# Retention attention with a PReLU feed-forward on one core: opening and block 1's units in another order

## The chip, the cores and the metric

The kernel runs on one core of a Trainium2 chip. Its engines are TensorE (PE, with weight loads shown apart as PEld), VectorE (DVE), ScalarE (ACT), GpSimd (POOL) and SyncE (SP); each works through its own instructions in order and waits on semaphores for the others. The metric is the device time of one execution in microseconds (us).

## The reference

Attention without softmax, with a decaying state, for 4 batches, 8 heads, 768 positions and 64 elements per head; its output, 3072 tokens by 512, goes through a feed-forward of width 2048 with a PReLU between.

```python
for t in range(S):                      # q, k, v: (4, 8, 768, 64), fp32
    state = gamma * state + outer(k[:, :, t], v[:, :, t])
    y[:, :, t] = (1 / sqrt(64)) * (q[:, :, t] @ state)
x = y.transpose(0, 2, 1, 3).reshape(3072, 512)
h = x @ w_in                            # (512, 2048)
g = maximum(h, 0) + alpha * minimum(h, 0)
out = g @ w_out                         # (2048, 512)
```

## The kernel before

The sequence is cut into chunks of 128 positions. A **unit** w is two chunks (256 positions) of four heads of one batch; `g = w % 2` is the half of the heads. There are 24 units in six **blocks** of four; the four units of a block give 512 tokens of x, which are the input of one feed-forward.

For a unit: `load` issues three transfers of 256 KB on SP's queue (k, q, v). `prep` multiplies k and q with decay factors into kdq (in the first two blocks k on DVE, q on POOL; unit 3's k on POOL too). `turn` transposes kdq in eight PE instructions into a PSUM tile (trb), and ACT copies it to kq; `cast_v` lets ACT convert v to vx. `scores` multiplies keys with queries into the PSUM tile sc (16 small PE instructions), `masked` lets DVE apply the causal mask (m). `state_sums` forms the chunk's sum of k times v (st), `state` adds the decayed state (ss, tg on DVE). `within` multiplies m with v into the PSUM tile y, followed by the products with the carried state that lie in the same row half; it ends with a tiny DVE memset that only tells that they are through. `finish` adds the carried products of the other half, which wait for that memset, and ACT copies y into xT. A `visit(old, new)` is within(old), scores and state_sums(new), finish(old), masked and state(new). From block 2 on, DMA transposes give kq instead of `turn`.

The feed-forward of a block is `ffn1`, 64 dense PE instructions of 128x512: 16 tiles (hps) of four steps hp, steps 0 and 1 reading the heads of g = 0 and steps 2 and 3 those of g = 1; each finished tile goes through ACT (hm) and DVE (gt). Then `ffn2`, again 64 dense instructions (ops): four tiles of 16 steps, each copied by ACT and stored. `tick(gen, m)` issues m of them, so that visits of the next block stand between them.

The order is written by hand (`manual_schedule`): every engine takes its instructions as the program's text issues them. PSUM tiles come from four tags: f and p with two buffers each, s (scores) and y with one of two banks each; a new tile waits until the old one's readers are done. `busy(m)` issues m products of ones (idle on PE) that nobody reads.

The opening is the work on block 0's four units, ahead of any dense work: loads, prep, turn and so on, with `get_wi` and `get_wo` on POOL's queue fetching the weights in four pieces each (win, wout). The loads of blocks 1 and 2 are issued after that; the first of them waits until the third piece of w_out has landed (`held`). In the opening, the loop for w = 1, 2, 3 runs busy(8), scores(w), state_sums(w), turn(w+1), finish(w-1), masked(w), state(w), within(w). Then come ffn1(0), the state sums of the later chunks of units 2 and 3, and ffn2(0) with block 1's turns and visits between its ticks.

Of the kernel before, what the change touches and what calls it, by code (L numbers as in the profile page):

```python
# [9 lines left out]
FP = mybir.dt.float32  # L10
# [8 lines left out]
def kernel(  # L19
# [15 lines left out]
    nc = tc.nc  # L35
    B, H, S, D = q.shape
    d_model, d_ff = moe_w_in.shape
    NFT = d_ff // 128
# [47 lines left out]
    alpha_sb = sbp.tile([NFT, 128], FP, tag="alpha", name="alpha")  # L86
    warm = sbp.tile([128, 128], FP, tag="warm", name="warm")[:, 0:1]
    ones = sbp.tile([128, 256], F16, tag="ones", name="ones")[:, 0:128]
    oma_sb = sbp.tile([128, 128], FP, tag="oma", name="oma")[:, 0:NFT]
    w_in_all = sbp.tile([128, NP, d_ff], F16, tag="win", name="win")  # L90
    w_out_all = sbp.tile([128, NFT, d_model], F16, tag="wout", name="wout")
# [43 lines left out]
    def load(w, which="kqv"):  # L135
        u, g, b, c3 = place(w)
        t = staged.setdefault(w, {})
        for nm in which:
            src = {"k": k, "q": q, "v": v}[nm]
            t[nm] = sbp.tile([128, 4, 2 * D], FP, tag=f"{nm}s", bufs=8, name=f"{nm}s{w}")  # L140
            ins = nc.sync.dma_start(
                out=t[nm],
                in_=src[b, 4 * g : 4 * g + 4, TU * c3 : TU * c3 + TU, :].rearrange(
                    "h (p a) d -> p h (a d)", a=2
                ),
            )
            if held:
                behind(ins, held.pop(), "loads of the second block after the weights")
# [34 lines left out]
    def busy(m):  # L183

        ips = ps("idle", "f")
        for _ in range(m):
            nc.tensor.matmul(  # L187
                out=ips[:, 0:128], lhsT=ones, rhs=ones, start=True, stop=True
            )

    def cast_v(w):
        nc.scalar.activation(  # L192
            out=prepped[w][2], in_=v_ins.pop(w), func=COPY, bias=0.0, scale=1.0
        )

    def turn(w, tag, fill=0, v_first=False):
        kdq, kq, vx = prepped[w]
        flat = kdq.rearrange("p k z r d -> p (k z r d)")
        trb = ps("trb", tag, 1024, F16)
        for i in range(8):  # L200
            if i == 4 and fill:
                busy(fill)
            nc.tensor.transpose(  # L203
                out=trb[:, 128 * i : 128 * i + 128],
                in_=flat[:, 128 * i : 128 * i + 128],
                identity=ident,
            )
        if v_first:
            cast_v(w)
        nc.scalar.activation(  # L210
            out=kq.rearrange("p b i -> p (b i)"),
            in_=trb[:, 0:1024],
            func=COPY,
            bias=0.0,
            scale=1.0,
        )
        if not v_first:
            cast_v(w)

    DIAG = [(0, 0), (1, 1), (0, 1), (1, 0)]  # L220

# [67 lines left out]
    def carried(w, y, started, same, after=None):  # L289
        u, g, b, c3 = place(w)  # L290
        kq = live[w][1]
        for x in range(2):
            for r in range(2):
                c = r if same else 1 - r
                if c3 + c == 0:
                    continue
                ins = nc.tensor.matmul(  # L297
                    out=y[half(x), 256 + 256 * c + 128 * r : 384 + 256 * c + 128 * r],
                    lhsT=tgs[2 * u + c, g][half(r), x, :],
                    rhs=kq[half(r), 4 + 2 * x : 6 + 2 * x, half(c)],  # L300
                    start=(c, x) not in started,
                    stop=(same == (c == r)),
                    skip_group_check=True,
                )
                started.add((c, x))
                if after is not None:
                    behind(ins, after, "the other row half wrote this bank")
                    after = None
        return ins

    def within(w):
        u, g, b, c3 = place(w)
        vx, m2 = live[w][2:4]
        y = ps("y", "y", 1024, FP, 1)
        started = set()
        for r in range(2):
            for a in range(2):
                for c, x in DIAG:
                    nc.tensor.matmul(  # L319
                        out=y[half(x), 256 + 256 * c + 128 * r : 384 + 256 * c + 128 * r],  # L320
                        lhsT=vx[half(c), 2 * r + x, a, :],
                        rhs=m2[half(c), 2 * r + x, a, :],
                        start=(c, x) not in started,
                        stop=(a == 1 and c3 + c == 0),
                        skip_group_check=True,
                    )
                    started.add((c, x))
        last = carried(w, y, started, True)
        done = nc.vector.memset(warm[0:1], 0.0)  # L329
        behind(done, last, "tells that the products within the chunks are through")  # L330
        live[w].append((y, started, done))

    def finish(w):
        u, g, b, c3 = place(w)
        y, started, done = live[w].pop()
        carried(w, y, started, False, done)
        live.pop(w)
        n, i = divmod(u, 2)
        if w % WB == 0:
            xT[n] = sbp.tile([128, 2, 4, 2, 128], F16, tag="xT", bufs=2, name=f"xT{n}")  # L340
        nc.scalar.activation(  # L341
            out=xT[n][:, g, 2 * i : 2 * i + 2].rearrange("p c r (i a) -> p (c r) i a", a=2),
            in_=y[:, 256:768].rearrange("p (s a i) -> p s i a", a=2, i=64),
            func=COPY,
            bias=0.0,
            scale=1.0,
        )
# [15 lines left out]
    def prelu(gt, ft, hps, lo, hi, hm):  # L363
        nc.vector.scalar_tensor_tensor(  # L364
            out=gt[:, ft, lo:hi],
            in0=hm,
            scalar=oma_sb[:, ft : ft + 1],
            in1=hps,
            op0=MULT,
            op1=ADD,  # L370
        )

    def minus(hps):
        hm = sbp.tile([128, TB], FP, tag="hm", bufs=3, name="hm")
        nc.scalar.activation(out=hm, in_=hps, func=RELU, bias=0.0, scale=-1.0)  # L375
        return hm

    def ffn1(n, order="spyfSpYf"):
        gt = sbp.tile([128, NFT, TB], F16, tag="gt", bufs=2, name=f"gt{n}")
        gts[n] = gt  # L380
        banks = Banks(order)
        for ft in range(NFT):
            hps = banks.next("hps")
            for hp in range(NP):
                nc.tensor.matmul(  # L385
                    out=hps,
                    lhsT=w_in_all[:, hp, 128 * ft : 128 * ft + 128],
                    rhs=xT[n][:, hp // 2, :, hp % 2, :],
                    start=(hp == 0),
                    stop=(hp == NP - 1),  # L390
                )
                if hp == NP - 1:
                    prelu(gt, ft, hps, 0, TB, minus(hps))
                yield

    def ffn2(n, parts=1, order="f"):
        gt = gts.pop(n)
# [30 lines left out]
    nc.scalar.dma_start(out=tab, in_=tab_h.ap())  # L428
    nc.scalar.dma_start(out=mi, in_=mi_h.ap())
    nc.scalar.dma_start(out=alpha_sb, in_=moe_alpha.rearrange("(ft p) -> ft p", p=128))  # L430
    for w, which in ((0, "kqv"), (1, "kq"), (2, "kq"), (1, "v"), (3, "kq"), (2, "v"), (3, "v")):
        load(w, which)
    nc.vector.memset(warm, 0.0)  # L433
    nc.scalar.activation(out=warm, in_=warm, func=RELU, bias=0.0, scale=-1.0)

    wi = moe_w_in.rearrange("(hp p) d -> p hp d", p=128)
# [9 lines left out]

    busy(34)
    prep(0, opening=True)
    turn(0, "f", 12)
    prep(1, opening=True)  # L450
    busy(16)
    scores(0)
    state_sums(0)
    masked(0)
    aps = ps("aps", "f")
    nc.tensor.transpose(out=aps[:, 0:NFT], in_=alpha_sb, identity=tab[0:NFT, ALT : ALT + NFT])
    prep(2, opening=True)
# [121 lines left out]
```

## Time and profile before

| | us |
|---|---|
| median of 3 runs | 225.86 (224.89 to 225.87) |
| the profiled execution | 225.53 |
| its span in the trace | 223.8 |
| mean granted PE clock | 0.969 of full |
| PE busy | 210.0 (94%) |
| DVE busy | 128.7 (58%) |
| ACT busy | 99.0 (44%) |
| POOL busy | 58.2 (26%) |

The profile is that of one execution. Times in it count from the span's start. In a timeline row stand the start, the length, the engine, the line, the operation, what is written and read, and in brackets how long the engine had been idle and what ended that. An engine name with a q (SPq, POOLq) is the engine's queue issuing a transfer. In the rows of the DMA view the last number is the time from issue to landing. The busy time of PE includes the drain of each instruction, so that 64 dense instructions show 380 ns each while they follow each other 216 ns apart.

### The profile page before, as it was taken

The numbers are of one execution on the slowest core, as the hardware profiler recorded it, in microseconds if no ns is written. First come the engines' busy times: TensorE is split into PE (matmuls) and PEld (weight loads), VectorE is DVE, ScalarE is ACT, GpSimd is POOL, SyncE is SP. The second block draws the span as 40 slices with busy tenths as digits, with TensorE's granted clock in tenths as the row PEclk, the third lists the DMA queues.
The fourth block names the chain that finished last, engine by engine and source line by source line (L and its number), as shares of the span: only waits on it lengthen the run. The fifth ranks groups of instructions, "written<-read, shape, count | busy, mean of one in ns | idle before, by whom it ended". The sixth has DMA issues, their size and how long they took to land.

```text
span 223.8 us, 5215 instructions
## 1 busy us (share of the span) xinstructions
PE 210.0 (94%) x2183; PEld 107.1 (48%) x2183; DVE 128.7 (58%) x226; ACT 99.0 (44%) x162; POOL 58.2 (26%) x69
## 2 busy tenths in 40 slices
PE   8666899999789999999999999999999999999993
PEld 8555544446434454444455444455444555444441
DVE  1653268955558896338874468936188773388000
ACT  2533256435656722266621376423376332576121
POOL 1593000369604580434502244400000000000000
PEclk9995589999999999999999999999999999999999
DMA  6959999999549969399427599031450012100112
GB/s 200 347 109 206 205 194 231 314 321 316 185 107 248 274 178 210 130 242 238 124 70 214 100 219 317 26 94 51 115 124 0 0 50 96 48 0 0 50 61 79
DMA packets 62935, 34.08 MB, mean 152 GB/s; under 512 B 18736, under 2 KB 59840, under 8 KB 62912
## 3 DMA queue, kind: packets, MB, share of 16 engines
q1 hardware_dynamic: 58368, 29.37, 48.3%
q0 software_dynamic: 4224, 4.19, 11.5%
q8 instruction: 17, 0.28, 0.5%
q10 hardware_dynamic: 320, 0.19, 0.3%
q14 instruction: 6, 0.05, 0.1%
HBM read 27.45 MB, written 6.29 MB: 151 GB/s over the span
## 4 chain that ended last, share of the span: by engine, by line
PE 89%; DVE 5%; ACT 3%; issue 0%; DVEq 0%
PE hps L385 38%; PE ops L406 36%; PE idle L187 4%; PE y L319 4%; PE sc L233 3%; DVE m L268 3%; PE trb L203 2%; PE y L297 2%; ACT kq L210 1%; PE st L257 1%; DVE tg L286 1%; ACT xT L341 1%; DVE kdq L158 1%; ACT vx L192 0%; DVE ss L283 0%
## 5 line engine op out<-in xcount | busy, mean ns | idle before, releaser
L364 DVE SCALAR_TENSOR_TENSOR gt<-hm,oma,hps 128x512 f16<-128x512 f32 x96 | 71.7, 747 | 32.1 <-ACT hm L375 21.7
L406 PE MATMUL ops<-wout,gt 128*128 128x512 f16 x384 | 89.2, 380 | 0.0
L385 PE MATMUL hps<-xT,win 128*128 128x512 f16 x384 | 85.8, 385 | 0.2 <-ACT xT L341 0.2
L375 ACT ACTIVATE hm<-hps 128x512 f32<-128x512 f32 x96 | 57.3, 597 | 28.6 <-PE hps L385 28.6
L385 PEld LDWEIGHTS <-win 128*128 128x128 f16 x384 | 37.9, 99 | 46.6 <-issue 2.6
L406 PEld LDWEIGHTS <-gt 128*128 128x128 f16 x384 | 35.2, 98 | 39.7
L268 DVE TENSOR_TENSOR m<-sc,mi 128x1024 f16<-128x1024 f32 x24 | 29.3, 1223 | 8.6 <-PE sc L233 6.7
L158 POOL TENSOR_TENSOR kdq<-qs,tab 128x512 f16<-128x512 f32 x24 | 25.8, 1075 | 31.5 <-DMA qs<-in_q_dram 30.3
L341 ACT ACTIVATE xT<-y 128x512 f16<-128x512 f32 x24 | 14.3, 597 | 43.4 <-PE y L297 40.7
L158 POOL TENSOR_TENSOR kdq<-ks,tab 128x512 f16<-128x512 f32 x17 | 17.9, 1054 | 52.1 <-DMA ks<-in_k_dram 43.0
L415 ACT ACTIVATE os<-ops 128x512 f32<-128x512 f32 x24 | 14.3, 597 | 33.4 <-PE ops L406 33.4
L329 DVE MEMSET warm<- 1x1 f32 x24 | 1.4, 59 | 29.6 <-PE y L297 29.6
L319 PE MATMUL y<-m,vx 64*64 64x128 f16 x384 | 10.5, 229 | 5.2 <-ACT xT L341 3.8
L210 ACT ACTIVATE kq<-trb 128x1024 f16<-128x1024 f16 x8 | 8.2, 1023 | 13.8 <-PE trb L203 13.8
L297 PE MATMUL y<-kq,tg 64*64 64x128 f16 x160 | 12.0, 237 | 1.8 <-DVE tg L286 1.2
L319 PEld LDWEIGHTS <-vx 64*64 64x64 f16 x384 | 6.8, 110 | 14.1 <-issue 11.0
L286 DVE TENSOR_TENSOR tg<-ss,tab 128x128 f16<-128x128 f32 x32 | 11.4, 355 | 1.1
L187 PE MATMUL idle<-ones 128*128 128x128 f16 x102 | 10.4, 278 | 1.1 <-DVE warm L433 1.1
L233 PE MATMUL sc<-kq 64*64 64x128 f16 x384 | 10.3, 224 | 0.3 <-ACT kq L210 0.2
L178 POOL CAST vx<-vs 128x512 f16<-128x512 f32 x16 | 9.8, 615 | 0.3 <-DMA vs<-in_v_dram 0.3
L283 DVE TENSOR_TENSOR ss<-tg,st 128x128 f32<-128x128 f16 x32 | 9.0, 282 | 1.5
L187 PEld LDWEIGHTS <-ones 128*128 128x128 f16 x102 | 8.8, 129 | 1.6 <-DVE warm L433 1.1
(22 smaller groups left out, 59.8 us busy)
## 6 DMA issues: line engine op xcount, KB each, us to landing
ks<-in_k_dram SPq DMA_DIRECT2D x24, 256.0 KB, 4.3
qs<-in_q_dram SPq DMA_DIRECT2D x24, 256.0 KB, 4.2
vs<-in_v_dram SPq DMA_DIRECT2D x24, 256.0 KB, 4.4
out_dram<-os SPq DMA_DIRECT2D x24, 256.0 KB, 2.3
win<-in_moe_w_in_dram POOLq DMA_DIRECT2D x4, 512.0 KB, 9.0
wout<-in_moe_w_out_dram POOLq DMA_DIRECT2D x4, 512.0 KB, 16.7
kq<-kdq SPq DMA_TRANSPOSE x16, 3.6
mi<-mi_const ACTq DMA_DIRECT2D x1, 128.0 KB, 2.9
```

The source lines that it names most:

```text
L158: eng.tensor_tensor(out=kdq[:, kind].rearrange("p z r d -> p r z d"), in0=src.rearrange("p (r x) (a d) -> p r (x a) d", a=2, x=2), in1=tab ...
L187: nc.tensor.matmul(out=ips[:, 0:128], lhsT=ones, rhs=ones, start=True, stop=True)
L233: nc.tensor.matmul(out=sc[half(c), at : at + 128], lhsT=kq[half(r), 2 * x + a, half(c)], rhs=kq[half(r), 4 + 2 * x : 6 + 2 * x, half(c)], ...
L268: nc.vector.tensor_tensor(out=m2.rearrange("p s a i -> p s (a i)"), in0=sc.rearrange("p (s n) -> p s n", n=256), in1=mask.unsqueeze(1).to_ ...
L297: ins = nc.tensor.matmul(out=y[half(x), 256 + 256 * c + 128 * r : 384 + 256 * c + 128 * r], lhsT=tgs[2 * u + c, g][half(r), x, :], rhs=kq[ ...
L319: nc.tensor.matmul(out=y[half(x), 256 + 256 * c + 128 * r : 384 + 256 * c + 128 * r], lhsT=vx[half(c), 2 * r + x, a, :], rhs=m2[half(c), 2 ...
L341: nc.scalar.activation(out=xT[n][:, g, 2 * i : 2 * i + 2].rearrange("p c r (i a) -> p (c r) i a", a=2), in_=y[:, 256:768].rearrange("p (s ...
L364: nc.vector.scalar_tensor_tensor(out=gt[:, ft, lo:hi], in0=hm, scalar=oma_sb[:, ft : ft + 1], in1=hps, op0=MULT, op1=ADD,)
L375: nc.scalar.activation(out=hm, in_=hps, func=RELU, bias=0.0, scale=-1.0)
L385: nc.tensor.matmul(out=hps, lhsT=w_in_all[:, hp, 128 * ft : 128 * ft + 128], rhs=xT[n][:, hp // 2, :, hp % 2, :], start=(hp == 0), stop=(h ...
L406: nc.tensor.matmul(out=opss[tq], lhsT=gt[:, ft, 128 * tq : 128 * tq + 128], rhs=w_out_all[:, ft, :], start=(ft == 0), stop=(ft == NFT - 1),)
L415: nc.scalar.activation(out=os_sb, in_=opss[tq], func=COPY, bias=0.0, scale=1.0)
```

## The change

The order in which instructions are issued changes, and with it the waits; the result is formed from the same products. In the opening the loads go unit by unit; scores(w) are issued ahead of within(w - 1) (unit 1's scores follow within(0) directly); the first piece of w_in is fetched ahead of unit 3's prep; cast_v is called apart from turn, mostly after finish; unit 2's `within` tells ACT instead of DVE that it is through (`teller`, a copy of one element). The fillers number 78 instead of 102. ffn1(0) begins with the steps of g = 0 of its first four tiles (`lead=4`): two of these inside within(3) (`mid`), two before finish(3), four after it; its tiles take their banks in another order. Block 1 gets other tick counts: units 6 and 7 are prepared later, turn(7) stands ahead of visit(5, 6), and unit 7 is finished with three dense instructions left. The code of blocks 2 to 5 is as before.

```diff
@@ load order @@
-    for w, which in ((0, "kqv"), (1, "kq"), (2, "kq"), (1, "v"), (3, "kq"), (2, "v"), (3, "v")):
-        load(w, which)
+    for w in range(WB):
+        load(w)
@@ turn no longer calls cast_v @@
-    def turn(w, tag, fill=0, v_first=False):
+    def turn(w, tag, fill=0):
...
-        if v_first:
-            cast_v(w)
...
-        if not v_first:
-            cast_v(w)
@@ within @@
-    def within(w):
+    def within(w, mid=None, teller=None):
...
+        if mid:
+            mid()
         last = carried(w, y, started, True)
-        done = nc.vector.memset(warm[0:1], 0.0)
+        if teller is None:
+            done = nc.vector.memset(warm[0:1], 0.0)
+        else:
+            done = teller.activation(
+                out=word[0:1], in_=word[0:1], func=COPY, bias=0.0, scale=1.0
+            )
@@ ffn1 @@
-    def ffn1(n, order="spyfSpYf"):
+    def ffn1(n, order="spyfSpYf", lead=0):
...
-        for ft in range(NFT):
-            hps = banks.next("hps")
-            for hp in range(NP):
...
+        hpss = {}
+        steps = [(ft, hp) for ft in range(lead) for hp in range(2)]
+        steps += [(ft, hp) for ft in range(lead) for hp in range(2, NP)]
+        steps += [(ft, hp) for ft in range(lead, NFT) for hp in range(NP)]
+        for ft, hp in steps:
+            if hp == 0:
+                hpss[ft] = banks.next("hps")
...
@@ opening @@
-    turn(0, "f", 12)
+    turn(0, "f", 8)
+    cast_v(0)
     prep(1, opening=True)
-    busy(16)
+    busy(12)
...
     prep(2, opening=True)
+    get_wi(0)
...
     turn(1, "f")
+    cast_v(1)
     within(0)
     prep(3, opening=True, k_on=nc.gpsimd)
-    for i in range(4):
+    for i in range(1, 4):
         get_wi(i)
...
-    for w in range(1, WB):
-        busy(8)
-        scores(w)
-        state_sums(w, (0,) if w > 1 else None)
-        if w + 1 < WB:
-            turn(w + 1, "f")
-        finish(w - 1)
-        masked(w)
-        state(w, (0,) if w > 1 else None)
-        within(w)
+    scores(1)
+    turn(2, "f")
+    finish(0)
+    cast_v(2)
+    state_sums(1)
+    masked(1)
+    state(1)
     busy(8)
+    scores(2)
+    within(1)
+    masked(2)
+    turn(3, "f")
+    finish(1)
+    cast_v(3)
+    state_sums(2, (0,))
+    state(2, (0,))
+    busy(8)
+    scores(3)
+    within(2, teller=nc.scalar)
+    masked(3)
+    state_sums(3, (0,))
+    finish(2)
+    state(3, (0,))
+    busy(8)
+    gen = ffn1(0, "ffspypSY", 4)
+    within(3, mid=lambda: tick(gen, 2))
+    tick(gen, 2)
     finish(3)
-    busy(8)
...
-    for _ in ffn1(0):
+    for _ in gen:
         pass
@@ block 1 @@
-    for w in range(WB, 2 * WB):
-        prep(w, opening=True)
-    tick(gen, 30)
-    turn(4, "p", v_first=True)
+    prep(4, opening=True)
+    prep(5, opening=True)
+    tick(gen, 21)
+    cast_v(4)
+    turn(4, "p")
+    tick(gen, 6)
+    visit(None, 4)
+    prep(6, opening=True)
+    tick(gen, 3)
+    cast_v(5)
+    turn(5, "p")
     tick(gen, 5)
-    visit(None, 4)
+    visit(4, 5)
+    prep(7, opening=True)
+    tick(gen, 3)
+    cast_v(6)
+    turn(6, "p")
+    tick(gen, 5)
+    cast_v(7)
+    turn(7, "p")
+    visit(5, 6)
     tick(gen, 8)
-    turn(5, "p", v_first=True)
-    tick(gen, 6)
-    visit(4, 5)
-    tick(gen, 1)
-    turn(6, "p", v_first=True)
-    tick(gen, 5)
-    visit(5, 6)
-    turn(7, "p", v_first=True)
-    tick(gen, 5)
     visit(6, 7)
+    tick(gen, 8)
+    within(7)
+    tick(gen, 2)
+    finish(7)
     for _ in gen:
         pass
-    visit(7, None)
```

More of the change, by code (lines that the diff above doesn't have):

```diff
@@ L88 @@
     ones = sbp.tile([128, 256], F16, tag="ones", name="ones")[:, 0:128]
+    word = sbp.tile([128, 128], FP, tag="word", name="word")[:, 0:1]
     oma_sb = sbp.tile([128, 128], FP, tag="oma", name="oma")[:, 0:NFT]
@@ L381, in ffn1 @@
         banks = Banks(order)
-        for ft in range(NFT):
-            hps = banks.next("hps")
-            for hp in range(NP):
[L385 to L394, printed above, removed]
+        hpss = {}
[5 more added lines that the diff above has]
+                hpss[ft] = banks.next("hps")
+            nc.tensor.matmul(
+                out=hpss[ft],
+                lhsT=w_in_all[:, hp, 128 * ft : 128 * ft + 128],
+                rhs=xT[n][:, hp // 2, :, hp % 2, :],
+                start=(hp == 0),
+                stop=(hp == NP - 1),
+            )
+            if hp == NP - 1:
+                prelu(gt, ft, hpss[ft], 0, TB, minus(hpss.pop(ft)))
+            yield
     def ffn2(n, parts=1, order="f"):
@@ L430 @@
     nc.scalar.dma_start(out=alpha_sb, in_=moe_alpha.rearrange("(ft p) -> ft p", p=128))
-    for w, which in ((0, "kqv"), (1, "kq"), (2, "kq"), (1, "v"), (3, "kq"), (2, "v"), (3, "v")):
-        load(w, which)
+    for w in range(WB):
+        load(w)
     nc.vector.memset(warm, 0.0)
+    nc.vector.memset(word, 0.0)
     nc.scalar.activation(out=warm, in_=warm, func=RELU, bias=0.0, scale=-1.0)
```

## The prediction, made before the changed kernel had run

> **What bounds the kernel now.** I read the engine shares first, then the chain of waits, then the waits of the tensor engine, and last the timeline of the first 65 us.
>
> ```profile
> span 223.8 us, 5215 instructions
> PE 210.0 (94%) x2183; PEld 107.1 (48%) x2183; DVE 128.7 (58%) x226; ACT 99.0 (44%) x162; POOL 58.2 (26%) x69
> 26.36 15.53 PE hps L385 x64
> 42.26 6.58 PE ops L406 x30
> 48.84 0.45 PE trb L203 x8
> 64.95 13.56 PE hps L385 x62
> 110.62 0.43 PE ops L406 x2
> 128.62 13.81 PE hps L385 x64
> 206.09 13.83 PE ops L406 x64
> ```
>
> The columns of the chain are start, length, what. From 64.95 us to the end the chain is the tensor engine (PE) back to back: 64 dense products take 13.81 us, 0.216 us each, whether of the first (hps) or second (ops) product. Nothing there is touched, so the change is worth what it does before 64.95. Two products of block 1's first tile had already run when the 62 began, so dense work of block 1 starts, in effect, at 64.95 - 2 x 0.216 = 64.5. I call that the mark. Behind it lie 223.8 - 64.5 = 159.3 us.
>
> Ahead of the mark two things cost time. A later block needs 128.62 - 110.62 = 18.0 us from its first ops to the next hps; block 0's ffn2 needs 64.5 - 42.26 = 22.2. Four transposition groups (0.45 each, block 1 only) explain 1.8, so about 2.4 us are waits. And the dense work does not start before 26 us.
>
> ```profile
> PE y L319 <- ACT xT L341: 3.8, 2, 1.9
> PE y L319 <- DVE m L268: 1.4, 3, 1.0
> PE trb L203 <- DVE tg L286: 1.3, 1, 1.3
> 9.20:12.60 3.40, 2.02 (x67) 1.68 (x66) 3.03 (x8) 1.54 (x2) 2.91 (x3) 1.00 0.97 286
> 12.60:16.00 3.40, 1.46 (x40) 1.12 (x41) 1.65 (x5) 2.03 (x3) 3.40 (x6) 1.00 0.37 53
> 22.90:26.30 3.40, 2.96 (x41) 2.51 (x42) 0.93 (x4) 0.68 (x2) 0.00 (x0) 0.50 1.24 206
> 26.30:29.70 3.40, 3.40 (x10) 1.20 (x9) 0.75 (x1) 0.60 (x1) 0.00 (x0) 0.50 1.22 195
> 29.70:33.10 3.40, 3.40 (x18) 1.50 (x17) 2.28 (x4) 2.39 (x4) 0.00 (x0) 1.00 1.22 198
> ```
>
> First the waits (total, times, longest), then the windows: after the window's length come the busy times of PE, PEld, DVE, ACT and POOL, then the granted PE clock, the DMA share and GB/s. The longest waits are `within` (y L319) for xT on ScalarE (ACT). After the thin window 12.6 to 16.0 (PE busy 1.46 us) the clock is granted at 0.50, and it comes back only after a window that is all dense work: 10 dense matmuls started from 26.3 to 29.7, against 18 in the next window. That is (18 - 10) x 0.216 = 1.7 us lost.
>
> **The opening, step by step.** These rows of the timeline (start, length, engine, line, what) carry it:
>
> ```profile
> 6.84 0.69 DVE L158 TENSOR_TENSOR kdq<-ks,tab 128x512 f16<-128x512 f32 x1 [2.28 <-DMA ks<-in_k_dram]
> 7.71 1.43 SPq L141 DMA_DIRECT2D vs<-in_v_dram  x2
> 9.15 1.04 POOL L158 TENSOR_TENSOR kdq<-qs,tab 128x512 f16<-128x512 f32 x1 [0.46 <-DMA qs<-in_q_dram]
> 9.27 1.47 DVE L158 TENSOR_TENSOR kdq<-ks,tab 128x512 f16<-128x512 f32 x1
> 10.66 0.28 DVE L286 TENSOR_TENSOR tg<-st,tab 128x128 f16<-128x128 f32 x1
> 10.68 1.04 POOL L158 TENSOR_TENSOR kdq<-ks,tab 128x512 f16<-128x512 f32 x1 [0.49 <-DMA ks<-in_k_dram]
> 11.17 0.62 PE L187 MATMUL idle<-ones 128*128 128x128 f16 x8
> 11.72 0.42 PE L233 MATMUL sc<-kq 64*64 64x128 f16 x16
> 12.85 1.02 ACT L210 ACTIVATE kq<-trb 128x1024 f16<-128x1024 f16 x1 [2.07 <-PE trb L203]
> 13.78 0.62 ACT L192 ACTIVATE vx<-vs 128x512 f16<-128x512 f32 x1
> 14.29 0.59 ACT L341 ACTIVATE xT<-y 128x512 f16<-128x512 f32 x1
> 14.93 0.42 PE L319 MATMUL y<-m,vx 64*64 64x128 f16 x16 [1.94 <-ACT xT L341]
> 15.89 0.54 PE L233 MATMUL sc<-kq 64*64 64x128 f16 x16
> 21.36 0.64 PE L233 MATMUL sc<-kq 64*64 64x128 f16 x16
> vs<-in_v_dram SPq DMA_DIRECT2D x1, 256.0 KB, 5.3
> L268 DVE TENSOR_TENSOR m<-sc,mi 128x1024 f16<-128x1024 f32 x24 | 29.3, 1223 | 8.6 <-PE sc L233 6.7
> L364 DVE SCALAR_TENSOR_TENSOR gt<-hm,oma,hps 128x512 f16<-128x512 f32 x96 | 71.7, 747 | 32.1 <-ACT hm L375 21.7
> ```
>
> Before, each unit is a closed loop: scores, transposes of the next, kq, vx, xT, and only then `within`, behind which the next scores stand. sc of unit 2 starts at 15.89, of unit 3 at 21.36.
>
> 1. Load order. k and q of units 2 and 3 move one slot back on SyncE's queue. Slots are 0.76 apart: POOL's q2 is released by its load at 9.15 and k3, two slots on, at 10.68. q2 now arrives near 9.9. DVE's k2 multiply took 1.47 beside POOL's q2 and 0.69 alone (6.84); now it runs 9.35 to 10.05, ahead of POOL. Bounds: nothing to -0.78 on the first tg; I take -0.6. So `within(0)` is through near 10.4, not 11.2. The Trainium skill ("GPSIMD Engine Reference", section Specifications) says that GpSimd's SBUF interfaces are shared with VectorE for instructions with two SBUF inputs; the two lengths agree.
> 2. The 8 fillers behind `within(0)` go (0.55 on the path, 11.17 to 11.72). sc1 at 10.4 to 10.5.
> 3. Transposes of unit 2 directly behind: q2 (9.9 + 1.04) sets them, through at 11.25. kq2 11.3 to 12.35 (1.02). masked(1), 1.22 from about 11.2, frees the score banks at 12.4. sc2 starts at 12.5, not 15.89, since it no longer stands behind `within(1)`, which waits for xT.
> 4. ACT now goes kq2, xT0, vx2: xT0 ends at 13.0 instead of 14.88, so within(1) runs at 13.05 instead of 14.93.
> 5. Unit 3: q3 is the 11th load. Before, the 11th was a v, issued at 7.71 and landed 5.3 later, 13.0 (window around that issue). POOL (k3 first, then q3, 1.04) ends at 14.1, transposes at 14.4, kq3 at 15.5. sc3 at 15.6, not 21.36. Then ACT sets the pace: xT1 0.59 to 16.15, vx3 0.62 to 16.8, the teller behind it (not in this trace; it copies one element: between nothing and xT's 0.59, I take 0.2, nearer to nothing), carried products, xT2 17.35 to 17.95, within(3) 18.0. What queues behind the teller on ACT is only xT2.
> 6. The first two dense matmuls at 18.3, two more behind, the rest from 19.35: four more on the finished half of xT (0.86) cover xT3 (0.59 and its release). So 60 x 0.216 = 12.95 from 19.35 gives 32.3. Four lead tiles finish 0.43 apart while DVE needs 0.747 for each, so banks come free late: bounds 0 and 4 x (0.747 - 0.43) = 1.3; I take 0.8. Dense part ends at 33.1, with the state sums 33.35, against 42.26: 8.9 earlier. Fillers fall by 24, but that they keep the clock is the first rival.
>
> **Weights and loads.** The stream of weights now decides the loads of block 1, held behind wo's third piece.
>
> ```profile
> 12.72 3.17 POOL L441 DMA_DIRECT2D win<-in_moe_w_in_dram  x4
> win<-in_moe_w_in_dram POOLq DMA_DIRECT2D x1, 512.0 KB, 5.6
> 34.90 0.37 SPq L141 DMA_DIRECT2D ks<-in_k_dram  x1
> 35.86 0.51 SPq L141 DMA_DIRECT2D vs<-in_v_dram  x1
> vs<-in_v_dram SPq DMA_DIRECT2D x1, 256.0 KB, 4.9
> ```
>
> The first piece is issued at 12.72 and lands at 18.3; the seventh releases SyncE at 34.90: 6 pieces in 16.6, 2.8 each. After, piece 1 goes out behind q2 at 10.95 (its issue, about 0.8, pushes k3 to 11.7, which q3's landing hides), the other seven behind q3 at 14.1. If the stream never pauses, the release is 10.95 + 22.2 = 33.1; if it restarts, 14.1 + 22.2 - 2.8 = 33.5. I take 33.4. win piece 2, needed at 22.5, is there by 20; wo's last piece by 36.2, needed at 33.35 + 12 x 0.216 = 35.9: about 0.3 exposed at worst.
>
> **Block 1.** PE alone needs 18.0 + 1.8 = 19.8, ending at 53.15. But the queue of DVE is now hung on v4: 33.4 + 0.96 (issued that much behind k4) + 4.9 = 39.25; vx4 0.62 and kq4 1.02 to 40.95; scores 0.46; m4 1.22 to 42.65; ss and tg with gaps 0.65 to 43.3; k6's multiply, between 0.69 and 1.47 beside POOL's q6, I take 1.25, to 44.55; m5 and its state 1.95 to 46.5; k7 0.69 to 47.2; transposes of 7 0.45; kq7 behind the end of vx7 1.25 to 48.9; then 21 dense matmuls (4.5) and the attention work of one and a half visits, (18.0 - 13.8) / 4 = 1.05 each, 1.6: 55.0. The new tick counts put work under each turn, so the old 1.3 us wait of a transposition for tg does not come back. Between 53.15 and 55.7 I take 55.0 for the mark. Dense products 62 to 64 cover xT7.
>
> **Sum.** 64.5 - 55.0 = 9.5. Span 223.8 - 9.5 = 214.3. The profiled execution took 225.53, 1.73 beyond its span; its median of three is 225.86, within 0.2%. So 214.3 + 1.7 = 216.0 us.
>
> **Rivals.** (a) The clock falls again in the opening. For it: 24 fillers fewer. Against: the window 9.2 to 12.6 kept the clock with 2.02 us of PE work; by the steps above every 3.4 us of the new opening holds over 2.2. If it falls, up to two windows (6.8 us) run at half speed: up to 3 us on ffn1's end. Scores of 4 then reach PE at 33.35 + 27 x 0.216 + 0.45 = 39.6 while kq4 ends at 40.95, so 1.35 is hidden: mark near 56.6, time 217.6. The Trainium skill ("TensorE: Matmul & The Clock Gate", Part 4: PE-mode transpose) says that transposes don't count as busy in the same way; by it the new opening, whose eight-transpose groups fill gaps, would be thinner and this rival likelier. By rows, the window that kept the clock had no more fillers than the new windows have, so I leave the chance where they put it; what the window's measure counts no row here shows.
>
> (b) The weights land no earlier, SyncE is released at 34.9 as before, and the chain hung on v4 moves by 1.5: mark 56.5, time 217.5. For it: the transfers share the DMA engines with the last loads; against: before, they lay nearly idle in 12.6 to 16.0 (DMA share 0.37, the last column but one).
>
> (c) k6 and v4 come easily and PE alone bounds block 1: mark 53.15 to 53.6, time about 214.3.
>
> (d) Slower than before: the clock stays at half through ffn1(0) and into ffn2(0). 60 matmuls at 0.431 from 20.0 end at 45.9, block 1 (19.8) at 66: 227, and each matmul of ffn2(0) at half adds 0.216, to 241 for all. It decides once the half clock lasts beyond about 45 us. Against: before, it came back after one dense window (29.7).
>
> **How the numbers follow.** Chances: forecast 0.70, (a) 0.13, (b) 0.08, (c) 0.05, (d) 0.04. The range goes from (c) with the bank waits gone, 53.15 - 0.8 and so 213.4, to (a) and part of (b) together, 218.4; only (d) and odd mixes lie outside. About 0.5%, 1.1 us, is what a measurement here can tell from no change: faster 0.95, same 0.01, slower 0.04.
>
> **What would show it.** Scores of units 2 and 3 near 12.5 and 15.6; first dense matmul near 18.3 at a granted clock of 1.00 throughout; state sums ending near 33.3; SyncE's first load of block 1 at 33.4; the mark at 55. A granted 0.50 in any window from 12 to 30 is (a); a mark that follows the first load one for one confirms the chain on v4; a dense stretch that idles for win or wout proves the weights' part wrong.

## The result: 217.44 us instead of 225.38

| kernel | median (lowest to highest), us | ratio to before, 95% interval |
|---|---|---|
| before | 225.38 (223.27 to 225.87) | |
| changed | 217.44 (217.35 to 217.66) | 0.9667 [0.9602, 0.9731] |

The change makes the kernel 3.3% faster, inside the range of the prediction and 1.4 us above its point. Ratios here and below leave disturbed executions out; medians are over all of a kernel's runs.

The page of the changed kernel (span, engines, granted clock in 40 slices, and the shares of the chain of work that ended last, by engine and by line):

```profile
span 215.7 us, 5170 instructions
PE 205.8 (95%) x2159; PEld 102.5 (48%) x2159; DVE 128.5 (60%) x226; ACT 99.2 (46%) x163; POOL 57.5 (27%) x69
PEclk9999999999999999999999999999999999999999
PE 76%; DMA 13%; SPq 4%; POOL 3%; DVE 1%; ACT 1%; issue 1%
PE ops L415 36%; PE hps L394 32%; DMA wout<-in_moe_w_out_dram 8%; DMA qs<-in_q_dram 5%; SPq L142 4%; PE y L316 3%; PE sc L230 2%; PE y L294 1%; PE st L254 1%; POOL win L451 1%; POOL kdq L159 1%; POOL wout L455 1%; DVE m L265 1%; DVE tg L283 0%; ACT kq L209 0%
```

The profiled execution took 217.43 us, 1.73 beyond its span, as before. The clock is full in every slice. Before, TensorE held 89% of the chain; now it holds 76%, and transfers 13%. Rows of the chain in order of time (start, length, what):

```profile
7.92 5.33 DMA qs<-in_q_dram
13.32 1.04 POOL kdq L159
14.36 2.24 POOL win L451 x3
16.60 1.43 POOL wout L455 x2
18.03 16.27 DMA wout<-in_moe_w_out_dram
34.32 0.37 SPq L142
...
36.49 5.38 DMA qs<-in_q_dram
41.94 1.05 POOL kdq L159
...
45.19 1.23 DVE m L265
46.65 1.07 DVE tg L283
47.72 0.61 DVE kdq L159
48.38 0.64 PE trb L204 x8
49.04 1.03 ACT kq L209
...
56.85 13.81 PE hps L394 x64
```

Read down: q of unit 3 arrives, GpSimd scales it and only then issues the other weights; the third piece of wo lands at 34.30; SyncE then starts block 1's loads; q of unit 5 arrives; and scalings, masks and copies lead to block 1's first dense product at 56.85, the mark (before: 64.5). The 16 us of dense work between 18 and 34 are not in this chain: they lie beside a transfer that ends later.

The opening in the timeline of the changed kernel (start, length, engine, line, what; the brackets hold idle time before it and what ended it):

```profile
12.73 0.42 PE L230 MATMUL sc<-kq 64*64 64x128 f16 x16 [0.26 <-DVE tg L283]
13.21 0.42 PE L316 MATMUL y<-m,vx 64*64 64x128 f16 x16
15.93 0.42 PE L230 MATMUL sc<-kq 64*64 64x128 f16 x16 [0.26 <-ACT kq L209]
18.50 0.60 PE L394 MATMUL hps<-xT,win 128*128 128x512 f16 x2
12.60:16.00 3.40, 2.54 (x64) 1.84 (x68) 2.52 (x7) 2.23 (x5) 3.20 (x5) 1.00 1.09 157
26.30:29.70 3.40, 3.40 (x18) 1.57 (x16) 2.71 (x4) 2.34 (x4) 0.00 (x0) 1.00 1.24 199
```

The last two rows are windows, with the columns of the prediction. Scores of unit 2 stand ahead of unit 1's products with v, as meant; scores of unit 3 run at 15.93 instead of 21.36; the thin window of before, with 1.46 us of PE work, now holds 2.54, and ten dense matmuls at half clock have become eighteen at full. In TensorE's waits the 3.8 us of y for xT are gone:

```profile
PE trb L204 <- DVE kdq L159: 0.7, 1, 0.7
PE st L254 <- ACT kq L209: 0.5, 1, 0.5
PE ops L415 <- DMA wout<-in_moe_w_out_dram: 0.4, 1, 0.4
```

### The profile page after: what moved, and what is told of

The parts are those of the page before. It is cut to its first block, busy times and chain, and to the rows that moved or that the text cites. A ratio compares the mean times of both kernels' runs of the same rounds, so it can differ in the third digit from the quotient of the medians.

```text
span 215.7 us, 5170 instructions
## 1 busy us (share of the span) xinstructions
PE 205.8 (95%) x2159; PEld 102.5 (48%) x2159; DVE 128.5 (60%) x226; ACT 99.2 (46%) x163; POOL 57.5 (27%) x69
## 4 chain that ended last, share of the span: by engine, by line
PE 76%; DMA 13%; SPq 4%; POOL 3%; DVE 1%; ACT 1%; issue 1%
PE ops L415 36%; PE hps L394 32%; DMA wout<-in_moe_w_out_dram 8%; DMA qs<-in_q_dram 5%; SPq L142 4%; PE y L316 3%; PE sc L230 2%; PE y L294 1%; PE st L254 1%; POOL win L451 1%; POOL kdq L159 1%; POOL wout L455 1%; DVE m L265 1%; DVE tg L283 0%; ACT kq L209 0%
## 5 line engine op out<-in xcount | busy, mean ns | idle before, releaser
L368 DVE SCALAR_TENSOR_TENSOR gt<-hm,oma,hps 128x512 f16<-128x512 f32 x96 | 71.2, 747 | 29.6 <-ACT hm L379 20.0
L394 PE MATMUL hps<-xT,win 128*128 128x512 f16 x384 | 84.4, 379 | 0.2 <-DVE gt L368 0.2
L379 ACT ACTIVATE hm<-hps 128x512 f32<-128x512 f32 x96 | 57.0, 597 | 25.5 <-PE hps L394 25.4
L394 PEld LDWEIGHTS <-win 128*128 128x128 f16 x384 | 37.3, 98 | 45.2 <-issue 0.5
L159 POOL TENSOR_TENSOR kdq<-qs,tab 128x512 f16<-128x512 f32 x24 | 25.1, 1047 | 31.6 <-DMA qs<-in_q_dram 31.6
L283 DVE TENSOR_TENSOR tg<-ss,tab 128x128 f16<-128x128 f32 x32 | 13.0, 407 | 1.1
L294 PE MATMUL y<-kq,tg 64*64 64x128 f16 x160 | 11.4, 228 | 0.5 <-DVE tg L283 0.5
L159 DVE TENSOR_TENSOR kdq<-ks,tab 128x512 f16<-128x512 f32 x7 | 4.8, 688 | 9.9 <-DMA ks<-in_k_dram 9.9
L316 PE MATMUL y<-m,vx 64*64 64x128 f16 x384 | 10.0, 222 | 0.3
L230 PEld LDWEIGHTS <-kq 64*64 64x64 f16 x384 | 6.8, 107 | 3.9 <-ACT kq L209 2.1
```

The costliest lines, as they stand in the source:

```text
L159: eng.tensor_tensor(out=kdq[:, kind].rearrange("p z r d -> p r z d"), in0=src.rearrange("p (r x) (a d) -> p r (x a) d", a=2, x=2), in1=tab ...
L230: nc.tensor.matmul(out=sc[half(c), at : at + 128], lhsT=kq[half(r), 2 * x + a, half(c)], rhs=kq[half(r), 4 + 2 * x : 6 + 2 * x, half(c)], ...
L283: nc.vector.tensor_tensor(out=tg, in0=stv, in1=decay, op=MULT)
L294: ins = nc.tensor.matmul(out=y[half(x), 256 + 256 * c + 128 * r : 384 + 256 * c + 128 * r], lhsT=tgs[2 * u + c, g][half(r), x, :], rhs=kq[ ...
L316: nc.tensor.matmul(out=y[half(x), 256 + 256 * c + 128 * r : 384 + 256 * c + 128 * r], lhsT=vx[half(c), 2 * r + x, a, :], rhs=m2[half(c), 2 ...
L368: nc.vector.scalar_tensor_tensor(out=gt[:, ft, lo:hi], in0=hm, scalar=oma_sb[:, ft : ft + 1], in1=hps, op0=MULT, op1=ADD,)
```

## Experiments

One table serves all of them. "First load" is the issue of block 1's first load on SyncE, "mark" the start of block 1's dense work in the chain (where the chain shows 62 products there, 0.43 less), both from one profiled execution. Each ratio is to before timed beside that kernel. The profiled execution isn't always near the median: block1_only's took 221.83 us, hold3's 221.43, lead0's 221.57. Expectations that put the changed kernel's mark at 56.6 go by its first product's own record (56.68).

| kernel | median (lowest to highest), us | ratio to before | first load | mark | between |
|---|---|---|---|---|---|
| before | | | 34.90 | 64.5 | 29.6 |
| block1_only | 225.05 (221.83 to 227.12) | 0.9996 [0.9946, 1.0046] | 36.01 | 61.3 | 25.3 |
| before_filled | 221.24 (220.96 to 222.00) | 0.983 [0.9777, 0.9882] | 35.54 | 60.5 | 25.0 |
| open_only | 219.16 (218.72 to 219.76) | 0.9734 [0.9680, 0.9788] | 34.27 | 58.0 | 23.8 |
| no_fill | 219.17 (218.09 to 219.94) | 0.9729 [0.9666, 0.9792] | 34.86 | 58.0 | 23.2 |
| changed | 217.44 (217.35 to 217.66) | 0.9667 [0.9602, 0.9731] | 34.32 | 56.9 | 22.5 |
| hold1 | 217.25 (216.82 to 217.65) | 0.9654 [0.9588, 0.9719] | 32.63 | 56.7 | 24.1 |
| hold3 | 220.21 (219.47 to 221.43) | 0.9791 [0.9719, 0.9862] | 38.57 | 60.9 | 22.3 |
| wi0_late | 221.21 (219.39 to 222.69) | 0.9803 [0.9717, 0.9889] | 38.47 | 60.9 | 22.4 |
| lead0 | 217.80 (216.37 to 221.57) | 0.9657 [0.9575, 0.9739] | 35.60 | 61.0 | 25.4 |
| q7_dve | 217.04 (216.14 to 217.86) | 0.9665 [0.9622, 0.9708] | 33.97 | 56.3 | 22.3 |
| k7_pool | 216.49 (216.10 to 218.85) | 0.9663 [0.9610, 0.9717] | 33.64 | 55.6 | 21.9 |
| k7_pool_turn | 217.46 (216.27 to 218.46) | 0.9685 [0.9647, 0.9724] | 35.27 | 56.6 | 21.3 |
| ticks_pool | 216.22 (215.34 to 216.93) | 0.9624 [0.9586, 0.9662] | 34.92 | 56.0 | 21.1 |

### Which half of the change carries the gain

**open_only**: the new opening with the old block 1 (all four units prepared ahead of the tiles, the old order of visits and old tile counts).

```diff
-    prep(4, opening=True)
-    prep(5, opening=True)
-    tick(gen, 21)
+    for w in range(WB, 2 * WB):
+        prep(w, opening=True)
+    tick(gen, 30)
...
-    visit(6, 7)
-    tick(gen, 8)
-    within(7)
-    tick(gen, 2)
-    finish(7)
+    visit(6, 7)
+    visit(7, None)
```

> The changed opening and ffn1(0), with block 1 in the old order (old tick counts, four preps at the head of it, cast_v ahead of each turn). Theory A (two separate gains; the opening brings dense work 8.5 us earlier, but what of it is kept depends on block 1 being paced by its loads, held behind the third piece of w_out): the old block 1 lets DVE multiply k4 to k7 before it masks unit 4, so unit 4 waits for k7's landing (near 45.7); mark (effective start of block 1's first hps) near 58.5 to 59.5 instead of 56.6, time 219.5 to 220.5, clock 1.00. Rival B (block 1's order hardly matters, the opening is everything): within 0.7 us of the changed kernel, 217.4 to 218.1.

219.16 us: theory A is right within half a microsecond, B falls. Behind the new opening the new block 1 is worth 1.7 us. Its chain shows what the new order takes away. First comes what theory A named: k of unit 7 lands at 45.70, VectorE scales it, and only then masks unit 4. Then come two more masks that nothing covers:

```profile
41.20 4.49 DMA ks<-in_k_dram
45.72 0.69 DVE kdq L159
46.41 1.13 DVE m L265
...
51.40 1.22 DVE m L265
52.62 0.21 DVE tg L283
...
55.24 1.22 DVE m L265
56.46 0.21 DVE tg L283
```

The changed kernel's chain has one mask in block 1 (45.19); from 50.48 on, tiles (`ops`) and attention products follow each other.

**block1_only**: the old opening with the new block 1, the same edit the other way round on the kernel before.

> The old opening and ffn1(0), with block 1 in the new order. Theory A: ffn2(0) starts at 42.2 as before, all loads of block 1 are there long before they are needed, and only the 2.4 us of waits inside block 1 can go: mark near 62.7, time 223.2 to 223.8; the clock at 0.50 from 16 to 30 as before. Rival B: no gain (225.4), since without an earlier opening the waits are only moved. Rival C (the new block 1 order brings as much as the opening): 221 or less.

225.05 us, no gain that can be measured: theory A missed, and the time is rival B's. The profiled execution, the fastest of the ten, has block 1 20.7 us long (40.59 to 61.26) where before had 22.2, so part of the gain is visible, but over ten timed runs it is lost in their spread of 5.3 us, which goes with the granted clock of the execution (mean 0.954 to 0.977). How much the new block 1 is worth behind the old opening stays open.

**before_filled**: the kernel before with fillers in its gaps and nothing else changed.

```diff
         state(w, (0,) if w > 1 else None)
+        busy(24 if w < 3 else 8)
         within(w)
```

> The kernel before, with 24 more fillers ahead of within(1) and within(2) and 8 ahead of within(3), where PE waited about 1.9, 1.9 and 1.0 us. Theory A (order and clock are two causes): with the clock kept at 1.00 the opening shortens by about 2.3 us and ffn1(0) by 1.7 to 1.9, so the mark is near 60.5 and the time 221.0 to 221.8; the other half of the gain of the changed opening is order alone. Rival D (the gain is the clock alone): the opening keeps its length in every respect but the clock, and this kernel comes to within 1 us of the changed one, 218.5. Rival E (fillers in the path cost what they bring): 225.5 or more.

221.24 us, as theory A said; D and E fall. The window that had 1.46 us of PE work has 2.90, the next keeps its clock, and the dense work takes 13.81 instead of 15.53 (rows: windows, then the chain):

```profile
12.60:16.00 3.40, 2.90 (x77) 2.59 (x75) 1.29 (x6) 1.91 (x3) 3.40 (x5) 1.00 0.36 32
16.00:19.40 3.40, 2.90 (x63) 2.57 (x60) 1.76 (x4) 2.03 (x3) 3.35 (x5) 1.00 1.22 202
23.49 13.81 PE hps L385 x64
```

So the gain splits, if the steps are taken in this order: 3.8 us for the clock alone (225.06, the median of before in these runs, to 221.24), 2.1 for the order of the opening (to 219.16), 1.7 for block 1 (to 217.44).

### Does the clock matter behind the new opening

**no_fill**: the changed kernel without its three groups of eight fillers.

```diff
-    busy(8)
     scores(2)
```
(and the same ahead of `scores(3)` and of `gen = ffn1(...)`)

> The changed kernel without its three groups of 8 fillers between 11.8 and 18 us. Theory A: PE is still busy with 1.6 us or more in every 3.4 us, near to the window that lost the clock in the kernel before (1.46), so the clock is about as likely lost as kept; if lost, ffn2(0) starts 2 to 2.5 us later, and most of that is hidden, because block 1 waits for its loads: mark 56.6 to 57.8, time 217.4 to 218.6. Rival F (a lost clock costs in full): 219.5 to 220.5 with a granted clock of 0.50 in two windows. If the clock stays at 1.00, no difference.

219.17 us, between the two, nearer to F. The clock falls for three windows of 3.4 us, from 13.57 to 23.81; two stretches of that time are these:

```profile
16.00:19.40 3.40, 2.25 (x59) 1.92 (x59) 2.64 (x6) 2.57 (x5) 3.40 (x5) 0.50 1.20 177
19.40:22.80 3.40, 3.09 (x29) 1.01 (x29) 0.24 (x2) 0.26 (x1) 1.05 (x2) 0.50 1.24 205
58.01 13.81 PE hps L394 x64
```

ffn2(0) starts 3.4 us later than in the changed kernel (37.11 against 33.73), the mark only 1.2 later: the rest is hidden behind block 1's loads. So the mechanism is theory A's, with ffn2(0) about 1 us later than it put. It is also rival (a) of the prediction, whose price of 1.6 us was about right: the 24 fillers are worth 1.7.

### Do the transfers set the mark

**hold3** and **hold1**: block 1's loads held behind the fourth, or behind the second, piece of wo instead of the third.

```diff
-    held.append(get_wo(2))      # hold3
-    get_wo(3)
+    get_wo(2)
+    held.append(get_wo(3))
```
(hold1 has `held.append(get_wo(1))` and plain calls for the pieces behind it.)

> The changed kernel, but the loads of blocks 1 and 2 wait for the fourth piece of w_out instead of the third: SyncE is released about 2.5 us later (36.85 instead of 34.3). Theory A (block 1 of the changed kernel is paced by its loads): the mark follows nearly one for one, +2.0 to +2.6 us, time 219.5 to 220.1. Rival G (block 1 is bound by PE and its own chains, and the loads only fill the cover): +0.8 us or less, 218.2 at most.

> The changed kernel, but the loads of blocks 1 and 2 wait for the second piece of w_out only, 2.6 us earlier than now (31.6). Theory A with free transfers: mark 1 to 1.5 us earlier, 216.0 to 216.5. Theory A with shared transfers (weights and loads use the same DMA engines): the last two pieces of w_out land 1.5 to 2.5 us later and ffn2(0), which needs the fourth after 12 dense matmuls, stalls for as much: 217.4 to 219.5. Rival G: 217.4, no change.

hold3: 220.21, about as theory A said; first load 4.25 later, mark 4.0 later, G falls. In that execution about 1.7 of the 4.25 came from a stream of weights that was itself later (its third piece of wo landed at 36.03 instead of 34.30). The clock also fell from 43.33 to 46.75, where six tiles took 2.56 us (1.29 in hold1), so it is partly chance that the two shifts agree so well. hold1: 217.25 against 217.44, nothing that can be told apart. Its first load goes out at 32.63 and lands 5.57 later, at 38.20, where the changed kernel's took 3.28 and landed at 37.60:

```profile
32.63 0.37 SPq L142 DMA_DIRECT2D ks<-in_k_dram  x1
...
34.94 2.16 SPq L142 DMA_DIRECT2D qs<-in_q_dram  x1
```

The fifth load's issue takes 2.16 us there, not 0.51. I read this as loads and weights sharing the same transfer engines: released into the running stream, the loads take longer. The trace bounds the rest only loosely, because this stream was itself 0.6 late (third piece of wo at 34.86 instead of 34.30): up to about half a microsecond of gain at the mark can hide there, far less than the 1.7 us by which the first load went out earlier.

**wi0_late**: the first piece of w_in issued with the others, behind q of unit 3.

```diff
-    get_wi(0)
...
-    for i in range(1, 4):
+    for i in range(4):
         get_wi(i)
```

> The changed kernel with the first piece of w_in fetched with the others, behind unit 3's prep, as in the kernel before. Theory A (the whole stream of weights then starts near 13.3): first piece lands near 19 to 19.9 instead of 16.6, dense work starts 0.7 to 1.4 us later, SyncE is released near 35.5 to 36.2, and the mark follows the release: +1.3 to +2.1, time 218.7 to 219.5. Rival H (the early piece matters to the first dense matmuls alone, and that is hidden in block 1): within 0.5 us of 217.4.

221.21 us, in theory A's direction and dearer than expected: 3.8 us; H falls. The dense work waits for w_in, the clock falls for two single windows (from 12.68 and from 22.92), and the first load moves to 38.47. A row of TensorE's waits, then three of the chain:

```profile
PE hps L394 <- DMA win<-in_moe_w_in_dram: 1.9, 1, 1.9
16.37 6.12 DMA win<-in_moe_w_in_dram
39.33 4.64 PE ops L415 x21
60.85 13.81 PE hps L394 x64
```

Behind the first piece of w_in this chain does not follow the loads: it is the dense work and the steps between its tiles, 5.6 us later at ffn2(0) than in the changed kernel (39.33 against 33.73), with the late loads close beside it. And part of the 3.8 us is not the line's. GpSimd was through with unit 3 at 16.37 here, 2.1 later than in the changed kernel (14.30); in hold3 and lead0, which do fetch the piece early, it was as late (16.31 and 16.12). Against hold3 the third piece of wo lands 2.4 later (38.45 instead of 36.03), and the lowest of the four times, 219.39, lies in the expected range. So I take the line to be worth 2 to 4 us. Without it the new load order, which brings q of unit 3 one slot later, delays the weights too: they would go out behind unit 3's products, at 14.30 in the changed kernel's execution, where before they did at 12.72.

**lead0**: no dense tiles begun with half the heads.

```diff
-    gen = ffn1(0, "ffspypSY", 4)
+    gen = ffn1(0, "ffspypSY", 0)
...
-    tick(gen, 2)
     finish(3)
```

> The changed kernel without the four led tiles: ffn1(0) takes its tiles one by one, two dense matmuls inside within(3), and the third waits for the last xT (near 20.65). Theory A: ffn1(0) ends 0.3 to 1.0 us later, which the wait for block 1's loads hides: 217.4 to 217.9. Rival I (the dense tiles begun with half the heads are worth their 1.3 us): 218.5 to 218.9.

217.8 us: theory A holds, I falls. The tiles begun with half the heads fill TensorE at 18.5 us, but in the changed kernel the chain there is the stream of weights, and they bring nothing measurable. The trace can't show this directly: its execution, the longest of the four, lost the clock from 16.66 to 26.90.

### What is left in block 1

**q7_dve**, **k7_pool**, **k7_pool_turn** and **ticks_pool** change unit 7's preparation (in q7_dve `prep` gets the parameter `q_on`); the last deals out the tiles anew as well.

```diff
-    prep(7, opening=True)
+    prep(7, opening=True, q_on=nc.vector)      # q7_dve
+    prep(7, opening=True, k_on=nc.gpsimd)      # the other three
...
-    cast_v(7)
     turn(7, "p")
+    cast_v(7)                                  # k7_pool_turn, ticks_pool
```

> The changed kernel with unit 7's product with q on VectorE, so that GpSimd does nothing from 45.3 us until block 2's products. Theory L (the decay step of L283, whose two inputs both lie in SBUF, takes 1.07 us at 46.65 instead of 0.29 because GpSimd's product with q runs from 46.53 to 47.57 and the two exclude each other): it takes 0.29 here, unit 7's products follow it by 0.69 each, and unit 7's transposes begin at about 48.3 as before, so the time stays at 217.2 to 217.8. Rival M (the step took long by its own wait for the state sums or by a slow VectorE): it stays at about 1.07, and the second product comes on top, 217.9 to 218.4. The Trainium skill (SBUF - State Buffer) says that a VectorE operation with two SBUF inputs and a GpSimd operation lock one port pair for the whole instruction, which is theory L.

> The changed kernel with unit 7's product with k on GpSimd alone. Theory A: the copy of unit 7's transposes still stands behind the cast of v, which waits for v7 (landed 48.26 us), so no gain although the wait of TensorE for VectorE's product goes: 217.2 to 217.8. Rival K (the product on VectorE behind the step of 1.07 us is what holds block 1, whatever stands behind it): 216.7 to 217.0.

> The changed kernel with unit 7's product with k on GpSimd and its transposes ahead of its v cast, the tiles dealt out as they were. Theory A: k7 lands at 45.65 us, GpSimd is through with both products at about 47.8 instead of VectorE at 48.3, the copy of the transposes no longer stands behind the cast of v (48.28 us), and it begins 0.5 us earlier than 49.04, so that unit 6's state sums do too: 216.8 to 217.1. Rival J: 217.2 to 217.7.

> The changed kernel with three edits in block 1: unit 7's product with k on GpSimd, its transposes ahead of its v cast, and the second dense part's tiles dealt out anew (23, 5, 5, 5, 2, 5, 2, 7, 6, 2 instead of 21, 6, 3, 5, 3, 5, 0, 8, 8, 2) so that tiles stand where the changed kernel's TensorE waited. Theory A (behind the weights, block 1's units are paced by their own transfers and by the scalings, and TensorE idles 0.74 us ahead of unit 7's transposes and 0.47 us ahead of unit 6's state sums, both at 48 to 50 us): most of these 1.2 us goes, the mark moves from 56.6 to 55.4-56.0, and the time is 216.1 to 216.8. Rival J (only the landing of the loads counts, and v7's at 48.3 us stands): the time stays at 217.2 to 217.7.

q7_dve settles why the decay step took 1.07 us. First the changed kernel's rows on VectorE and GpSimd, then this one's on VectorE, from their timelines:

```profile
46.65 1.07 DVE L283 TENSOR_TENSOR tg<-ss,tab 128x128 f16<-128x128 f32 x1
46.53 1.04 POOL L159 TENSOR_TENSOR kdq<-qs,tab 128x512 f16<-128x512 f32 x1 [1.25 <-DMA qs<-in_q_dram]
```

```profile
46.37 0.29 DVE L283 TENSOR_TENSOR tg<-ss,tab 128x128 f16<-128x128 f32 x1
46.58 0.69 DVE L159 TENSOR_TENSOR kdq<-ks,tab 128x512 f16<-128x512 f32 x1
47.18 0.69 DVE L159 TENSOR_TENSOR kdq<-qs,tab 128x512 f16<-128x512 f32 x1
```

With no product on GpSimd the step takes 0.29; beside one it ends at 47.72, just behind GpSimd's end at 47.57. Theory L holds, M falls, and the time stays (217.04, with a range that reaches from 216.14 to 217.86).

k7_pool was expected to bring nothing and came out at 216.49, nearer to rival K. But its profiled execution also had unit 7's v landed 12.3 us behind the first load, where the changed kernel's came after 13.9, so the cast that theory A counted on as the next wait was not late. Its range (216.10 to 218.85) covers both theories; it decides nothing. k7_pool_turn does not show the expected gain in time either (217.46), although its stretch from first load to mark is 1.2 us shorter than the changed kernel's: its loads began 0.95 later.

ticks_pool is the fastest kernel of the study: 216.22 us, all six runs (215.34 to 216.93) below the changed kernel's four. TensorE's waits for VectorE's product ahead of unit 7's transposes (0.7) and for the copy ahead of unit 6's state sums (0.5) are no longer among its longest, which are

```profile
PE trb L204 <- POOL kdq L159: 1.4, 2, 0.7
...
PE y L294 <- DVE tg L283: 0.6, 1, 0.6
PE sc L230 <- ACT kq L209: 0.4, 1, 0.4
```

Theory A's range holds it, and the mark of 56.03 stands 0.8 ahead of the changed kernel's although the first load was 0.6 later. ffn2(0) began 1.75 later too (35.48), and from 27.18 us to the mark the chain is almost all TensorE's: 20.6 us from the first ops to the mark. That the ratio beats the changed kernel's is likely and not shown: the two intervals, [0.9586, 0.9662] and [0.9602, 0.9731], overlap.

## Why the prediction was right, step by step

- **The opening.** Steps 1 to 6 came out in order, the first two on time (scores of unit 1 at 10.44), the others 0.2 to 0.6 us late: scores of unit 2 at 12.73 (12.5 forecast), of unit 3 at 15.93 (15.6), first dense product at 18.50 (18.3), the rest from 19.93 (19.35). The teller took 0.20, as taken. The dense part ended, and the state sums began, at 33.36 (33.1); ffn2(0) began at 33.73 (33.35). Part of the late start was given back: the last 60 products took 13.4 us, where 12.95 and 0.8 for bank waits were put.
- **Weights and loads.** The release came at 34.32, not 33.4. The first piece went out at 11.10 (10.95) and landed 5.5 later; the second went out at 14.30 (14.1) and needed 6.7 to land, where the forecast gave it 5.6 after the restart; in the other kernels that issue it there it took 5.4 to 6.5, so most of this miss belongs to the one execution. Rival (b), that the weights land hardly earlier than before, is half true: 0.6 us of the 1.5 expected (release at 34.32; 34.90 before). That the time lies near rival (b)'s 217.5 is chance in part, since the chain runs elsewhere. wo's last piece held TensorE for 0.38 us (at worst 0.3).
- **Block 1's chain.** The forecast hung it on v of unit 4. The chain shows q of unit 5, 36.49 to 41.87, GpSimd's product and the transposes behind it, so that the 48.9 forecast for unit 7's kq (50.07) rests on a path that another one overtook. Two sizes were wrong and nearly cancel: unit 6's product with k took 0.68 us (1.25 taken), because GpSimd began its product only at 44.24, when VectorE's was through, and is not in the chain; unit 5's mask and state took 2.53 (1.95 taken), because the decay step in them waited for GpSimd and took 1.07 instead of 0.29. The prediction read the 1.47 beside GpSimd as a slowdown. Its own rows show a wait: the product ended at 10.74, 0.55 behind GpSimd's end at 10.19. The Trainium skill ("SBUF — State Buffer", section SBUF: two separate sides) says that a VectorE operation with two SBUF inputs and a GpSimd operation that reads SBUF exclude each other for a whole instruction; the runs agree. So every such step beside GpSimd was to be looked for, not one.
- **The end of block 1.** From the end of unit 7's kq to the mark stood 6.1 us in the forecast; 50.07 to 56.85 is 6.8. The 21 tiles show as 4.95 in the chain instead of 4.5: each of the four stretches of dense work between attention pieces costs about 0.1 us more than its products. The attention work took 1.8 instead of 1.6.
- **The sum.** Mark: 56.85 - 55.0 = 1.85 late, of which 0.9 is the release, 0.25 the chain to unit 7's kq, 0.7 the end. Behind the mark the span has 158.85 us, 0.45 less than before, though the prediction took nothing to change there. It had read the old chain as TensorE back to back from the mark on; from 78.53 to 83.36 that chain lies on ScalarE and VectorE, in block 2's first unit, and in the changed kernel it does not. 1.85 - 0.45 = 1.4, the miss: 217.43 - 216.0. That the total came out 0.45 us nearer than the mark is luck.
- **The rivals.** (a) did not happen in the profiled execution, whose windows hold 2.62 us of PE work and more; no_fill shows that it is real and what it costs. The 2.02 us that kept the clock before were no safe bar, as the last section shows. Two other executions had a mean granted clock of 0.992, which is what one window of 3.4 us at half speed in 215.7 us gives; they took 217.46 and 217.35, so by this estimate a single lost window, wherever it lay, cost next to nothing. (c) did not come in the changed kernel; its 19.8 us for TensorE alone were too few, as ticks_pool's 20.6 and block1_only's 20.7 show. (d) did not come, and even no_fill's three windows at half speed stay far from it.
- **What the prediction had, and what it did not see.** It hung the mark on the release of the loads, and hold3 bears that out: later loads, later mark. From 8 to 42 us one line of transfers, loads, weights, loads, ends last in the changed kernel. But that line hardly moved: the release came only 0.6 us earlier than before. Nearly all of the 7.6 us at the mark is dense work that starts 8.5 us earlier and no longer lies in the way, until the loads do. What the prediction did not see is how close the next limit stands: in ticks_pool, no_fill, wi0_late and lead0, where ffn2(0) began at 35.48 or later, the chain from there to the mark runs on TensorE and the steps between its tiles, not on the loads.

## What to carry to other kernels

When a stage is moved ahead, look for what it was moved past: 8.5 us of earlier dense work became 7.6 us at the next stage's start, because block 1's loads, which hardly moved, had been ready before they were needed and then became the limit; with block 1's old order it was 6.5 (open_only). Releasing a transfer earlier into a stream that is already full brought nothing measurable here; issuing the stream's first piece earlier did. And of two engines that exclude each other, check each two-input step against the other's schedule, since which one waits is set by who begins first.

## What the runs showed of the hardware

**The lock works both ways.** In k7_pool, unit 6's product with k, 0.69 us by itself, began at 43.13, 0.16 behind GpSimd's product with q:

```profile
43.13 1.53 DVE L159 TENSOR_TENSOR kdq<-ks,tab 128x512 f16<-128x512 f32 x1
42.97 1.14 POOL L159 TENSOR_TENSOR kdq<-qs,tab 128x512 f16<-128x512 f32 x1 [1.25 <-DMA qs<-in_q_dram]
```

It ended at 44.66, 0.55 behind GpSimd's end at 44.11. In q7_dve the same product, begun at 43.55 and ended at 44.23, made GpSimd's, begun at 43.65, take 1.49 instead of 1.04.

**What loses the clock is not the busy time alone.** The granted clock changes at multiples of 3.41 us (at 13.57 and 23.81 in no_fill, three times 3.41 apart). Windows cut at such times, two of k7_pool_turn and one of before; behind the length stands PE's busy time:

```profile
7.96:11.37 3.41, 2.34 (x75) 1.54 (x67) 2.87 (x6) 1.69 (x3) 1.67 (x2) 1.00 1.13 334
11.37:14.78 3.41, 3.41 (x76) 2.79 (x68) 2.57 (x7) 2.19 (x4) 2.66 (x4) 0.50 0.79 166
```

```profile
9.22:12.64 3.42, 2.06 (x66) 1.70 (x66) 3.05 (x8) 1.54 (x2) 2.93 (x3) 1.00 0.96 283
```

The first lost the clock for the next window with 2.34 us of work; before kept it with 2.06. Leaving the transposes out gives 1.54 and 1.62, the right way round, but open_only kept the clock with 1.10 counted so (8.57 to 11.98). By the rule of the Trainium skill ("TensorE: Matmul & The Clock Gate", Part 4: PE-mode transpose) that the prediction named under rival (a), transposes don't count as busy in the same way; these windows neither bear it out nor refute it.

**The opening itself varies by one to two microseconds.** GpSimd issued the first piece of w_in at 11.10 us in the changed kernel's profiled execution and at 11.23 to 12.33 in those of the other kernels that issue it there, and the second piece, behind unit 3's products, at 14.30 and at 14.39 to 16.31, with the loads ahead of it landing later; the first load moves with it. Comparisons of less than 1 us between kernels of this study need more runs than they had.
